# Key features of two blocks: transposed by VectorE and moved by DMA inside SBUF instead of transposed by TensorE, in a fused attention and gated-FFN layer

## The chip, the cores and the metric

The kernel runs on one core of a Trainium2 chip. Its metric is the device time of one launch in microseconds. Before the change the median of three runs is 671.38 us (670.75 to 671.44). A profile is one execution of its own, recorded by the hardware profiler; its times are counted from the start of the recorded span.

## What is computed

A sequence of 2048 tokens with 448 features is normalised, and the result is `x + A(xn) + B(xn)`. `A` is an attention with 16 heads of 28 features that goes through four blocks of 512 tokens and carries a memory `M` and its normaliser `z` from block to block; `B` is a gated feed-forward layer with 1792 hidden features.

```python
xn = layernorm(x)
for s in range(4):                       # blocks of 512 tokens
    qs, ks, vs = q[:, :, s], k[:, :, s], v[:, :, s]
    a_dot = softmax(qs @ ks.T * scale + mask) @ vs
    pq = phi(qs)                         # t + 1 where t > 0, exp(t) elsewhere
    a_mem = (pq @ M) / (pq @ z + 1e-6)
    o = g * a_mem + (1 - g) * a_dot
    pk = phi(ks)
    M = M + pk.T @ vs                    # the memory update
    z = z + pk.sum(tokens)
out = x + concat(o) @ wo + (sigmoid(xn @ w_gate) * (xn @ w_up)) @ w_down
```

## The kernel before, in words

Every matrix product is done with split operands: a value is a high part (rounded by ScalarE's copy to the type that TensorE reads fast) and a low part (the value less its high part), and a product is 11 matmuls of 128 rows each, the list `TERMS`. `xs0` to `xs3` hold the normalised tokens of the four blocks, transposed, in 7 chunks: 0 to 2 are high parts of 128 features, 4 to 6 their low parts, and chunk 3 holds the high part of the last 64 features in its upper 64 partitions and the low part in the lower 64. So matmuls 2, 3, 5, 6, 8 and 9 of a product touch a low part of tokens or weights, and the last two take chunk 3.

There is a front stage (some 140 us), in which the memory path and the projections are done, and then the long stage in which gated matmuls and causal attention are woven into each other. The change is in the front stage. It goes through the blocks `b` = 0 to 3 in the order in which the code stands:

- `values(b, t)` (L400) makes the value rows of one tile of 128 tokens (11 matmuls into a bank `pv`, then a copy by ScalarE into `vst`). Four tiles make a block.
- `keys_queries(b, c)` (L407) projects chunk `c` of the 896 key and query columns (11 matmuls into a bank `pp`; ScalarE makes the high part and the exponential, VectorE the low part `qk` and the feature map `e`). Chunks 0 to 3 hold keys, 3 to 6 queries. `qk` is stored to HBM (`qd`) for the attention, and the query features `e` to `fd`.
- `key_rows(c, e)` (L430) turns a key chunk so that tokens lie on partitions: four transposes by TensorE into a bank `pk`, and a copy by ScalarE into `kn`.
- `update(b)` (L438) adds the block's keys times values to the memory: 64 small matmuls into a bank `pmm` (keys stationary), then four VectorE instructions, one for each strip of 32 partitions, into `mst`.
- `recall(b, phi)` (L462) reads the memory of the blocks so far for the queries of a block: 32 small matmuls from `phi`, which SyncE loads back from `fd` (`load_features`, L459).
- For blocks 2 and 3 the normalised tokens are transposed by VectorE in squares of 32 by 32 (L359, into a staging buffer that is the space of `phi` for block 2 and of `acc2` for block 3), spread by 16 DMAs (L374, half on the queue of SyncE, half on that of GpSimd) into `stage`, and then split by `split_strips` (L377): ScalarE makes the high part, VectorE the low part.
- For block 1 the tokens are normalised by VectorE (L350) and transposed by TensorE (`pt`, L103). `statistics(2)` (L587) works out mean and variance of block 2's rows on VectorE.

TensorE, ScalarE and VectorE do the front stage's instructions in the order of the code. GpSimd's and SyncE's are put in an order by the tile framework's scheduler. Each engine takes its own instructions strictly in order; so a DMA that waits on SyncE's queue holds all DMAs behind it.

Of the kernel before, what the change touches and what calls it, by code (L numbers as in the profile page):

```python
# [9 lines left out]
F32 = mybir.dt.float32  # L10
# [6 lines left out]
P = 128  # L17
# [47 lines left out]
FILLS = (2, 2)  # L65
WARM = 10
# [3 lines left out]
def kernel(  # L70
# [236 lines left out]
    with tc.tile_pool(name="front", bufs=2) as sb, tc.manual_schedule(engines=FRONT):  # L307
# [69 lines left out]
        def split_strips(b, k):  # L377

            if k < 3:
                A.activation(xs[b][:, k, :], stage[:, k, :], AF.Copy)  # L380
                V.tensor_sub(xs[b][:, 4 + k, :], stage[:, k, :], xs[b][:, k, :].bitcast(F32))
            else:
                A.activation(xs[b][:64, 3, :], stage[:64, 3, :], AF.Copy)
                V.tensor_sub(xs[b][64:, 3, :], stage[:64, 3, :], xs[b][:64, 3, :].bitcast(F32))
# [52 lines left out]

        def update(b):  # L438

            pmm = bank("pmm", "m")  # L440
            for j in range(HG):
                for t in range(NT):
                    for i in range(NG):
                        h = HG * i + j
                        T.matmul(pmm[32 * i:32 * i + DH, 32 * j:32 * j + 32], kn[:, t, DH * h:DH * (h + 1)],  # L445
                                 vst[:, t, h, :], start=t == 0, stop=t == NT - 1)
            p3 = pmm[:, :P].rearrange("p (j c) -> p j c", c=32)
            new, old = mst[(b + 1) % 2], mst[b % 2]
            for i in range(NG):
                strip = slice(32 * i, 32 * i + DH)  # L450
                if b == 0:
                    V.tensor_copy(new[strip], p3[strip])
                else:
                    V.tensor_add(new[strip], p3[strip], old[strip])
# [4 lines left out]
        def load_features(b, i, phi):  # L459
            nc.sync.dma_start(phi[32 * i:32 * i + DH], fd[b][i * GW:(i + 1) * GW].rearrange("(j r) n -> r j n", r=DH))  # L460
# [28 lines left out]
        nc.sync.dma_start(stage[:, 0:2, :], w_qk[0:2].rearrange("c p n -> p c n"))  # L489
        nc.sync.dma_start(stage[:, 2:4, :], w_qk[2:4].rearrange("c p n -> p c n"))  # L490
        raw_qk = [stage[:, c, :] for c in range(4)]
        for c in range(4, 6):
            raw_qk.append(two_k("wqk_raw"))
            nc.sync.dma_start(raw_qk[c], w_qk[c])
        nc.sync.dma_start(acc[1], x_block(1))
        raw_qk.append(four_k(F32, "wqk_raw")[:, 0, :])
        nc.sync.dma_start(raw_qk[6], w_qk[6])
# [12 lines left out]
        def split_qk(c):  # L510
            r = raw_qk[c].rearrange("p (c n) -> p c n", c=4)
            A.activation(wqk[c][:, 0:4, :], r, AF.Copy)
            G.tensor_sub(wqk[c][:, 4:8, :], r, wqk[c][:, 0:4, :].bitcast(F32))
# [59 lines left out]
        for b in range(NB):  # L573
# [6 lines left out]
            for t in range(3 if b == 0 else 0, NT):  # L580
                values(b, t)
                if b == 0:
                    split_qk(t)
# [18 lines left out]
            for k, c in enumerate((3, 4, 5, 6, 0, 1, 2) if last else range(7)):  # L602
# [9 lines left out]
                if b == 0 and c + 4 < 7:  # L612
                    split_qk(c + 4)
                if b == 2 and 0 < n < NG or last and 0 < n <= NG:
                    answer(b - 1, n - 1, ts)
                if b == 2 and k == 6:
                    answer(1, NG - 1, ts)
                if k == 0:
                    if b == 0:
                        st[1] = rstd(*st[1])  # L620
                    if b == 0:
                        A.activation(gate, gate, AF.Exp, scale=-1.0)
# [6 lines left out]
                if last:  # L629
# [4 lines left out]
                    for i in range(NG):  # L634
                        if k == (2, 3, 4, 4)[i]:
                            load_features(b, i, phi)
# [6 lines left out]
                if k == 6:  # L643
                    update(b)
# [29 lines left out]
    class Pair:  # L674
# [5 lines left out]
        def load(self):  # L680

            self.qk = sb.tile([P, 2, 2, L], F32R, name="qk2", bufs=2)
            for c, parts in enumerate(((0, 0), (1, 0), (0, 1))):
                for n in range(2):
                    r0 = D * (1 - n) + DH * self.h0
                    nc.sync.dma_start(self.qk[DH * c:DH * (c + 1), n].bitcast(F32),
                                      qd[self.s][r0:r0 + 2 * DH, parts[n], :].rearrange("(j p) f -> p j f", p=DH))
# [268 lines left out]
```

## Time and profile before

| | |
|---|---|
| median of three runs | 671.38 us |
| the profiled execution: its time, and its span | 671.5 us, 669.6 us |
| TensorE busy | 663.7 us, 99% of the span |
| VectorE, ScalarE, GpSimd busy | 571.4, 336.1 and 147.4 us |
| DMA, mean over the span | 132 GB/s |

A profile's page gives the busy time of each engine, the chain of work that ended last, and groups of equal instructions with their count, mean duration in ns and the idle time before them. Its views by time give the start and length of single instructions or of runs of equal ones. PE is TensorE, DVE VectorE, ACT ScalarE, POOL GpSimd; SPq is the queue on which SyncE issues DMAs. L412 is line 412 of the kernel.

### The profile page before, as it was taken

Reading aid. Unit: us, or ns where it says so; the run is one execution under the profiler, and the core shown is the slowest. Engines: PE = TensorE matmul, PEld = TensorE weight load, DVE = VectorE, ACT = ScalarE, POOL = GpSimd, SP = SyncE. Lnnn points to the kernel's source line nnn. Section 1 sums busy time; section 2 is a strip of 40 time slices with the busy share of each in tenths; the row PEclk is TensorE's granted clock in tenths of the full one; section 3 lists DMA queues with packets and bytes.
Section 4 is the critical chain, followed back from the end, with each engine's and each line's share of the span. In section 5 each row is a group of like instructions: output and inputs, shape, how many; then the busy total and the mean of one; then the engine's idle time right before and its main releaser. Section 6 shows DMA issues by size and latency. Waiting matters only on the chain.

```text
span 669.6 us, 11201 instructions
## 1 busy us (share of the span) xinstructions
PE 663.7 (99%) x3922; PEld 553.2 (83%) x3922; DVE 571.4 (85%) x987; ACT 336.1 (50%) x560; POOL 147.4 (22%) x354
## 2 busy tenths in 40 slices
PE   8999999999999999999999999999999999999997
PEld 7888888778888888788787878788887887888897
DVE  6986695878999899899998999899998997999864
ACT  4848474423556455455645546455544644545220
POOL 3502210002222222233122322222122122321000
PEclk9999999999999999999999999999999999999999
DMA  8537788995523432324243423426243352323442
GB/s 321 221 128 251 238 287 284 309 273 197 144 73 88 109 93 73 103 57 105 74 96 103 89 72 57 128 52 141 57 103 64 92 115 57 86 78 80 112 153 97
DMA packets 48767, 88.09 MB, mean 132 GB/s; under 512 B 6856, under 2 KB 22856, under 8 KB 48200
## 3 DMA queue, kind: packets, MB, share of 16 engines
q1 hardware_dynamic: 45048, 79.01, 39.1%
q0 software_dynamic: 3520, 8.26, 6.1%
q8 instruction: 31, 0.51, 0.3%
q14 instruction: 24, 0.20, 0.1%
q10 hardware_dynamic: 144, 0.11, 0.0%
HBM read 52.89 MB, written 32.64 MB: 128 GB/s over the span
## 4 chain that ended last, share of the span: by engine, by line
PE 97%; DVE 2%; DMA 0%; ACT 0%; issue 0%; DVEq 0%
PE pgu L260 42%; PE pd L184 21%; PE pp L412 11%; PE st L704 6%; PE pa L790 5%; PE po L889 5%; PE pv L392 5%; PE pk L434 1%; PE pmm L445 1%; PE n L467 1%; DMA acc<-in_x 0%; DVE stats L324 0%; PE pt L103 0%; DVE xn L350 0%; DVE xs L110 0%
## 5 line engine op out<-in xcount | busy, mean ns | idle before, releaser
L260 PE MATMUL pgu<-xs,wgu 128*128 128x512 f32 x1232 | 301.2, 392 | 0.0
L260 PEld LDWEIGHTS pgu<-xs,wgu 128*128 128x128 f32 x1232 | 228.7, 188 | 46.6 <-issue 2.5
L184 PE MATMUL pd<-wdn,hh 128*128 128x448 f32 x672 | 155.3, 366 | 0.0
L184 PEld LDWEIGHTS pd<-wdn,hh 128*128 128x128 f32 x672 | 122.7, 188 | 11.6 <-issue 0.8
L719 POOL TENSOR_SCALAR_AFFINE_SELECT w<-w 128x256 f32<-128x256 f32 (+1 forms) x160 | 76.1, 479 | 224.0 <-ACT w L708 157.6
L772 ACT ACTIVATE w<-w 128x1024 f32<-128x1024 f32 (+1 forms) x96 | 87.8, 915 | 58.3 <-DVE w L768 58.1
L708 ACT ACTIVATE w<-st 128x512 f32<-128x512 f32 x128 | 75.6, 592 | 60.1 <-PE st L704 59.8
L768 DVE TENSOR_TENSOR w<-w,mb 128x1024 f32<-128x1024 f32 (+1 forms) x96 | 100.6, 1054 | 0.8
L726 DVE TRANSPOSE_TENSOR_REDUCE mx<-w 128x32 f32<-128x1024 f32 x64 | 78.9, 1233 | 4.9 <-POOL w L719 4.9
L412 PE MATMUL pp<-xs,wqk 128*128 128x512 f32 x308 | 73.7, 393 | 0.2 <-DVE kn L473 0.2
L186 DVE TENSOR_TENSOR acc<-pd,acc 128x448 f32<-128x448 f32 x112 | 67.4, 602 | 4.0 <-PE pd L184 4.0
L283 ACT ACTIVATE hh<-sg 128x512 fp32r<-128x512 f32 x56 | 35.3, 631 | 67.7 <-DVE sg L277 44.6
L412 PEld LDWEIGHTS pp<-xs,wqk 128*128 128x128 f32 x308 | 57.2, 188 | 12.9 <-issue 0.8
L704 PE MATMUL st<-qk 84*128 84x128 f32 (+3 forms) x256 | 62.0, 313 | 0.0
L267 ACT ACTIVATE sg<-pgu 128x512 f32<-128x512 f32 x56 | 33.2, 592 | 45.0 <-PE pgu L260 44.9
L704 PEld LDWEIGHTS st<-qk 84*128 84x128 f32 x256 | 47.9, 189 | 8.7 <-issue 1.4
L277 DVE SCALAR_TENSOR_TENSOR sg<-sg,pgu 128x512 f32<-128x512 f32 x56 | 37.7, 673 | 10.1 <-PE pgu L260 9.9
L754 DVE STREAM_TRANSPOSE mb<-top 128x1024 f32<-128x1024 f32 x32 | 39.5, 1234 | 3.3 <-POOL top L751 3.2
L286 DVE SCALAR_TENSOR_TENSOR hh<-sg,hh 128x512 fp32r<-128x512 f32 x56 | 38.2, 681 | 0.2 <-ACT hh L283 0.2
L419 DVE TENSOR_TENSOR qk<-pp,qk 128x512 fp32r<-128x512 f32 x28 | 19.2, 686 | 22.2 <-ACT e L417 21.6
L790 PE MATMUL pa<-w,vv 128*32 128x128 f32 (+3 forms) x512 | 37.8, 436 | 0.0
L392 PE MATMUL pv<-wv,xs 128*128 128x448 f32 x176 | 37.4, 367 | 0.3 <-POOL wv L508 0.2
(113 smaller groups left out, 607.2 us busy)
## 6 DMA issues: line engine op xcount, KB each, us to landing
qk<-qd SPq DMA_DIRECT2D x192, 112.0 KB
qd<-qk SPq DMA_DIRECT2D x28, 512.0 KB
raw<-in_w_ffn SPq DMA_DIRECT2D x14, 512.0 KB
acc<-in_x SPq DMA_DIRECT2D x5, 896.0 KB
vd<-vst SPq DMA_DIRECT2D x4, 1024.0 KB
vv<-vd SPq DMA_DIRECT2D x16, 256.0 KB
od<-w POOLq DMA_DIRECT2D x16, 256.0 KB, 4.1
sums<-od SPq DMA_DIRECT2D x32, 128.0 KB
```

The lines of the kernel that those rows point to most:

```text
L184: T.matmul(pd[:, :D], l, r, start=n == 0, stop=n == len(mms) - 1)
L186: V.tensor_add(acc[b][:, t, :], pd[:, :D], acc[b][:, t, :])
L260: T.matmul(dst, wgu[f][:, w, side * P:(side + 1) * P], xs[b][:, a, :], start=n == 0, stop=n == len(TERMS) - 1)
L392: T.matmul(pv[:, :D], xs[b][:, a, t * P:(t + 1) * P], wv[w], start=n == 0, stop=n == len(TERMS) - 1)
L412: T.matmul(pp, wqk[c][:, w, :], xs[b][:, a, :], start=n == 0, stop=n == len(TERMS) - 1)
L704: T.matmul(st[:, at:at + L - kb * P], self.qk[:KS, 1, h, kb * P:(kb + 1) * P], self.qk[:KS, 0, h, kb * P:], start=True, stop=True)
L708: A.activation(w, st, AF.Copy)
L719: G.affine_select(d, d, pattern=pattern, base=0, channel_multiplier=-1, compare_op=ALU.is_ge, fill=MASK)
L726: V.tensor_reduce(self.mx[:, 32 * h:32 * h + 32], w3[:, h, :2 * L].rearrange("p (b n) -> p b n", n=32), axis=mybir.AxisListType.X, op=ALU. ...
L768: V.tensor_sub(w, w, m)
L772: A.activation(w, w, AF.Exp, scale=SCALE)
L790: T.matmul(pa[32 * j:32 * j + 32, kb * P:], self.vv[:, kb, 32 * j:32 * j + 32], self.pairs[j // 2].block(j % 2, kb), start=kb == 0, stop=k ...
```

## The change

For blocks 1 and 2 (`EXCHANGED`) the key chunks no longer go through TensorE. VectorE transposes each chunk in squares of 32 by 32 into the staging buffer of the block after next (free by then), and 24 DMAs a block, half of them on SyncE's queue and half on GpSimd's, bring the squares to the partitions where the tokens belong, into `kn_blocks`. So that a head's features lie in a few squares, the columns of the key and query weights are put in another order (feature first, head second), on the chip: the weights come in eight DMAs with pieces of 512 bytes, and `split_qk` reads them with a step of 28 elements. Loads of `qd` and `fd` follow the new order.

`update` now has the values stationary and the keys moving, with a step of 16 elements between them; the sum is kept transposed in `memory` and turned by VectorE into `mst`. For blocks 1 and 2 it is called after the matmuls of the next block's first value tile. The low parts in `split_strips` go from VectorE to GpSimd. `statistics(2)` moves from ahead of block 0's keys to behind its second chunk; `split_qk` and some calls of `answer` (the memory's part of the output) move by a chunk or so.

```diff
+EXCHANGED = (1, 2)
...
+        memory = sb.tile([P, HG, 32], F32, name="memory", bufs=1)
         kn = eight_k(F32, "kn").rearrange("p (t a) n -> p t (a n)", t=NT)
+        kn_blocks = kn.rearrange("p t n -> p (t n)")[:, :NT * D].rearrange("p (m t r) -> p m t r", t=NT, r=32)
...
             if k < 3:
                 A.activation(xs[b][:, k, :], stage[:, k, :], AF.Copy)
-                V.tensor_sub(xs[b][:, 4 + k, :], stage[:, k, :], xs[b][:, k, :].bitcast(F32))
+                G.tensor_sub(xs[b][:, 4 + k, :], stage[:, k, :], xs[b][:, k, :].bitcast(F32))
...
         def values(b, t):
             pv = bank("pv", "p")
             value_terms(b, t, pv, EARLY[1] if b == 0 else TERMS)
+            if t == 0 and b - 1 in EXCHANGED:
+                update(b - 1)
             store_values(b, t, pv)
...
+        def turned(b, c):
+
+            space = stages[b + 1].rearrange("p (c n) -> p c n", n=256)
+            return space[:, 2 * c:2 * c + 2, :].rearrange("p c n -> p (c n)")
+
+        def turn_keys(e, et):
+            rows = et.shape[0]
+            V.transpose(et.rearrange("p (q t r) -> p t q r", q=4, t=NT),
+                        e[:rows].rearrange("p (t q n) -> p t q n", q=4, t=NT))
+
+        def send_keys(b, et=None):
...
+            for q in range(4):
+                for i in range(4 if et is None else 2):
+                    queue = nc.sync if i % 2 else nc.gpsimd
...
+                        queue.dma_start(to[32 * q:32 * q + 32, i:12:4, :], src[strip, :, q, :])
...
+                        queue.dma_start(to[32 * q:32 * q + 32, 12 + i, :], et[strip, P * q:P * (q + 1)])
+
+        def exchange(b, c):
+            if c == 1:
+                turn_keys(e[0], turned(b, 0))
+            elif c == 2:
+                turn_keys(e[1], turned(b, 1))
+                turn_keys(e[2], turned(b, 2))
+                send_keys(b)
+            elif c == 3:
+                et = sb.tile([P, L], F32, name="e", bufs=4)
+                turn_keys(e[3], et[:64])
+                send_keys(b, et)
...
-                        T.matmul(pmm[32 * i:32 * i + DH, 32 * j:32 * j + 32], kn[:, t, DH * h:DH * (h + 1)],
-                                 vst[:, t, h, :], start=t == 0, stop=t == NT - 1)
...
+                        T.matmul(pmm[32 * i:32 * i + 32, 32 * j:32 * j + DH], vst[:, t, h, :], rows[t][h],
+                                 start=t == 0, stop=t == NT - 1)
...
+                V.tensor_add(m3, p3, m3)
+            V.transpose(mst[(b + 1) % 2].rearrange("p j c -> p (j c)"), memory.rearrange("p j c -> p (j c)"))
...
+                r = raw_qk[side].rearrange("p w (h r) -> p w r h", h=H)[:, :, r0:r1, :]
...
-                    st[2] = statistics(2, 0, NT)
...
+                if b == 0 and k == 1:
+                    st[2] = statistics(2, 0, NT)
...
-                if k in (3, 5):
+                if b in EXCHANGED:
+                    exchange(b, c)
+                elif k in (3, 5):
```

How this moves instructions shows in three places. The first is VectorE in block 0, at its second chunk: `qk` and `e` are that chunk's low part and feature map, `xn` the first normalised tile of block 1, `acc_71` the rows of block 2. Before:

```order
L625 TENSOR_SCALAR gate_n<-gate 128x4
L419 TENSOR_TENSOR qk<-pp,qk 128x512
L424 SCALAR_TENSOR_TENSOR e<-pp,e 128x512
L350 TENSOR_SCALAR xn<-acc_70,mv_327,y_338 128x16x7x4
L419 TENSOR_TENSOR qk<-pp,qk 128x512
```

And now:

```order
L424 TENSOR_TENSOR qk<-pp,qk 128x512
L429 SCALAR_TENSOR_TENSOR e<-pp,e 128x512
L327 BN_STATS stats_397<-acc_71 128x6
L328 BN_AGGR mv_398<-stats_397 128x2
L327 BN_STATS stats_397<-acc_71 128x6
L328 BN_AGGR mv_398<-stats_397 128x2
L327 BN_STATS stats_397<-acc_71 128x6
L328 BN_AGGR mv_398<-stats_397 128x2
L327 BN_STATS stats_397<-acc_71 128x6
L328 BN_AGGR mv_398<-stats_397 128x2
L329 TENSOR_SCALAR vh_399<-mv_398 128x4
L353 TENSOR_SCALAR xn<-acc_70,mv_327,y_338 128x16x7x4
```

Nine instructions of `statistics(2)` have come between the chunk's feature map and the first normalised tile of block 1.

The second place is GpSimd's queue, and TensorE's, from block 2 to block 3 (`acc_71` is now the staging buffer, `xs_68` the tokens of block 3, `od` the attention's output in HBM). GpSimd before:

```order
L374 DMA stage<-acc_71 32x4x128
L374 DMA stage<-acc_71 32x3x128
L479 DMA od_92<-tb 128x512 x2
L479 DMA od_92<-xn 128x512 x2
L479 DMA od_93<-tb 128x512 x2
```

GpSimd now:

```order
L377 DMA stage<-acc_71 32x4x128
L377 DMA stage<-acc_71 32x3x128
L523 DMA od_92<-tb 128x512
L384 TENSOR_TENSOR xs_68<-stage,xs_68 128x512 x2
L462 DMA kn<-acc_71 32x3x128 x8
L464 DMA kn<-e 32x128 x4
L523 DMA od_92<-tb 128x512
L384 TENSOR_TENSOR xs_68<-stage,xs_68 128x512
L387 TENSOR_TENSOR xs_68<-stage,xs_68 64x512
L523 DMA od_92<-xn 128x512 x2
```

Twelve DMAs of the keys stand between the second and the third low part of block 3's tokens, and one more DMA. From block 1 to block 2 the twelve stand between the first low part and the second. TensorE there before (`xs_67` is block 2):

```order
L412 MATMUL pp<-xs_67,wqk_117 128x512 x11
L434 MATMUL pk<-ident,e 128x128 x8
L412 MATMUL pp<-xs_67,wqk_118 128x512 x11
L412 MATMUL pp<-xs_67,wqk_119 128x512 x11
L434 MATMUL pk<-ident,e 128x128 x8
L412 MATMUL pp<-xs_67,wqk_120 128x512 x11
L445 MATMUL pmm<-vst,kn 28x32 x64
L392 MATMUL pv<-wv,xs_68 128x448 x44
```

TensorE now:

```order
L417 MATMUL pp<-xs_67,wqk_117 128x512 x11
L417 MATMUL pp<-xs_67,wqk_118 128x512 x11
L417 MATMUL pp<-xs_67,wqk_119 128x512 x11
L417 MATMUL pp<-xs_67,wqk_120 128x512 x11
L395 MATMUL pv<-wv,xs_68 128x448 x11
L490 MATMUL pmm<-kn,vst 32x28 x64
L395 MATMUL pv<-wv,xs_68 128x448 x33
```

The transposes `pk` are gone, and the first value tile of the next block has moved ahead of the update.

The third place is SyncE's queue from block 1 to block 2 (`fd_84` holds block 1's query features, `phi` their reloaded copy, `vd_89` block 2's values). Before:

```order
L427 DMA fd_84<-e 128x512
L460 DMA phi<-fd_84 28x4x512
L420 DMA qd_80<-qk 128x1024
L427 DMA fd_84<-e 128x512
L460 DMA phi<-fd_84 28x4x512 x3
L398 DMA vd_89<-vst 128x2048
L374 DMA stage<-acc_71 32x4x128
L374 DMA stage<-acc_71 32x3x128
```

And now:

```order
L432 DMA fd_84<-e 128x512
L425 DMA qd_80<-qk 128x1024
L432 DMA fd_84<-e 128x512
L377 DMA stage<-acc_71 32x4x128
L503 DMA phi<-fd_84 28x2048 x4
L401 DMA vd_89<-vst 128x2048
L377 DMA stage<-acc_71 32x3x128
```

The first DMA of block 3's token spread, which needs all four normalised and turned tiles of block 3, has moved ahead of the loads of `phi`.

More of the change, by code (lines that the diff above doesn't have):

```diff
@@ L444, in update @@
                         h = HG * i + j
-                        T.matmul(pmm[32 * i:32 * i + DH, 32 * j:32 * j + 32], kn[:, t, DH * h:DH * (h + 1)],
-                                 vst[:, t, h, :], start=t == 0, stop=t == NT - 1)
[L447 to L454, printed above, removed]
+                        T.matmul(pmm[32 * i:32 * i + 32, 32 * j:32 * j + DH], vst[:, t, h, :], rows[t][h],
+                                 start=t == 0, stop=t == NT - 1)
+            p3, m3 = pmm[:, :P].rearrange("p (j c) -> p j c", c=32)[:, :, :DH], memory[:, :, :DH]
+            if b == 0:
+                V.tensor_copy(m3, p3)
+            else:
+                V.tensor_add(m3, p3, m3)
+            V.transpose(mst[(b + 1) % 2].rearrange("p j c -> p (j c)"), memory.rearrange("p j c -> p (j c)"))
         def features():
@@ L459, in load_features @@
         def load_features(b, i, phi):
-            nc.sync.dma_start(phi[32 * i:32 * i + DH], fd[b][i * GW:(i + 1) * GW].rearrange("(j r) n -> r j n", r=DH))
+            nc.sync.dma_start(phi[32 * i:32 * i + DH],
+                              fd[b].rearrange("(r h) n -> r h n", h=H)[:, HG * i:HG * (i + 1), :])
         def recall(b, phi):
@@ L488 @@
         raw = [raw[t // 2][:, t % 2 * D:(t % 2 + 1) * D] for t in range(4)]
[L489 to L497, printed above, removed]
+        raw_qk = [space.rearrange("p t n -> p (t n)")[:, :4 * D].rearrange("p (w n) -> p w n", w=4)
+                  for space in (stage, features())]
+        for side in range(2):
+            for c in range(4):
+                to, at = (P * c, 0) if side == 0 else (max(P * c - 64, 0), 64 if c == 0 else 0)
+                n = min(P, D - to) if side == 0 else P - at
+                nc.sync.dma_start(raw_qk[side][:, :, to:to + n],
+                                  w_qk[c + 3 * side].rearrange("p (w n) -> p w n", w=4)[:, :, at:at + n])
+            if side == 0:
+                nc.sync.dma_start(acc[1], x_block(1))
         load_rows(2)
@@ L510, in split_qk @@
         def split_qk(c):
-            r = raw_qk[c].rearrange("p (c n) -> p c n", c=4)
-            A.activation(wqk[c][:, 0:4, :], r, AF.Copy)
-            G.tensor_sub(wqk[c][:, 4:8, :], r, wqk[c][:, 0:4, :].bitcast(F32))
+            for side in range(2):
+                j0, j1 = max(P * c, D * side), min(P * (c + 1), D * (side + 1))
+                if j0 >= j1:
+                    continue
+                r0, r1 = ((j - D * side) // H for j in (j0, j1))
+                r = raw_qk[side].rearrange("p w (h r) -> p w r h", h=H)[:, :, r0:r1, :]
+                hi, lo = (wqk[c][:, w:w + 4, j0 - P * c:j1 - P * c].rearrange("p w (r h) -> p w r h", h=H)
+                          for w in (0, 4))
+                A.activation(hi, r, AF.Copy)
+                G.tensor_sub(lo, r, hi.bitcast(F32))
         warm = bank("warm", "gu")
@@ L611 @@
                     turn_back(n2, ts, range(2, NG))
[L612 to L617, printed above, removed]
+                if b == 0 and c + 3 < 7:
+                    split_qk(c + 3)
+                if b == 0 and k == 1:
+                    st[2] = statistics(2, 0, NT)
+                if b == 2 and k in (1, 4, 5, 6):
+                    answer(1, max(k - 3, 0), ts)
+                if last and 0 < n <= NG:
+                    answer(2, n - 1, ts)
                 if k == 0:
@@ L633 @@
                         phi = features()
-                    for i in range(NG):
-                        if k == (2, 3, 4, 4)[i]:
-                            load_features(b, i, phi)
+                    for i in range(NG if k == 4 else 0):
+                        load_features(b, i, phi)
                     if k > 4:
@@ L684, in load @@
                 for n in range(2):
-                    r0 = D * (1 - n) + DH * self.h0
-                    nc.sync.dma_start(self.qk[DH * c:DH * (c + 1), n].bitcast(F32),
-                                      qd[self.s][r0:r0 + 2 * DH, parts[n], :].rearrange("(j p) f -> p j f", p=DH))
+                    rows = qd[self.s][D * (1 - n):D * (2 - n), parts[n], :].rearrange("(r h) f -> r h f", h=H)
+                    nc.sync.dma_start(self.qk[DH * c:DH * (c + 1), n].bitcast(F32), rows[:, self.h0:self.h0 + 2, :])
         def block(self, h, kb):
```

16 lines of the change are left out of this document (13 added, 3 removed).

## The prediction

> **What bounds the kernel now.** I read the page first: busy shares, then the shares of the chain that ended last.
>
> ```profile
> PE 663.7 (99%) x3922; PEld 553.2 (83%) x3922; DVE 571.4 (85%) x987; ACT 336.1 (50%) x560; POOL 147.4 (22%) x354
> PE 97%; DVE 2%; DMA 0%; ACT 0%; issue 0%; DVEq 0%
> ```
>
> TensorE is busy for 663.7 of 669.6 us and makes 97% of the chain. Each stall that the change puts into TensorE's order lengthens the kernel, and each TensorE instruction that goes shortens it, as long as nothing else is late in its place. Then the chain of waits in the front stage (start, length, what, both in us):
>
> ```profile
> 19.84 9.98 PE pp L412 x44
> 29.82 1.05 PE pk L434 x8
> 30.87 0.48 PE pt L103 x4
> ...
> 51.27 10.00 PE pp L412 x44
> 61.27 0.87 PE pk L434 x8
> ...
> 67.17 0.87 PE pk L434 x8
> 68.04 2.52 PE pp L412 x11
> 70.56 1.22 PE pmm L445 x82
> 71.78 9.07 PE pv L392 x44
> 80.85 2.52 PE pp L412 x11
> 83.37 1.15 PE n L467 x32
> ...
> 92.23 0.87 PE pk L434 x8
> ...
> 98.12 0.87 PE pk L434 x8
> ```
>
> One TensorE piece follows the other without a gap. A chunk of keys or queries takes 2.50 to 2.52 us, a value tile 9.07/4 = 2.27, a matmul of it 0.21. So TensorE's clock is the clock of the front stage, and the question is which operand comes too late for it once the change is in.
>
> **What goes.** The four groups of `pk` in blocks 1 and 2, 0.87 us each, all on the chain: **-3.5 us**. That they do go is seen in TensorE's order, so "the change does nothing" is no case here. The update keeps its 64 matmuls.
>
> **Block 0: statistics(2) ahead of a normalised tile.** Rows of the timeline (VectorE, then ScalarE):
>
> ```profile
> 21.34 0.62 DVE L324 BATCH_NORM_STATS2 stats<-acc 128x6 f32<-128x448 f32 x1
> ...
> 24.39 0.17 DVE L326 TENSOR_SCALAR vh<-mv 128x4 f32<-128x4 f32 x1
> 24.59 0.69 DVE L419 TENSOR_TENSOR qk<-pp,qk 128x512 fp32r<-128x512 f32 x1
> ...
> 30.08 0.50 DVE L350 TENSOR_SCALAR xn<-acc,mv,y 128x448 f32<-128x448 f32 x1
> 23.55 0.59 ACT L417 ACTIVATE e<-pp 128x512 f32<-128x512 f32 x1
> ```
>
> The nine instructions hold VectorE from 21.34 to 24.59, 3.25 us. At their old place they delayed only L419, which could have begun when ScalarE's L417 ended (24.14): leaving gains at most 0.45. At the new place they stand straight ahead of L350 at 30.08. TensorE's `pt` at 30.87 needs that tile, ready at 30.58: 0.29 us of slack. Behind the waiting `pt` stands all of TensorE. 3.25 - 0.45 - 0.29 = **+2.5 us**; between 1.0 (if VectorE makes up more of its backlog earlier) and 3.2 (if the early gain isn't realised).
>
> **The low parts on GpSimd, at block 2's first value tile.**
>
> ```profile
> 60.60 0.69 DVE L424 SCALAR_TENSOR_TENSOR e<-pp,e 128x512 f32<-128x512 f32 x1
> L513 POOL TENSOR_TENSOR wqk<-stage,wqk 128x512 fp32r<-128x512 f32 x4 | 5.1, 1297 | 4.8 <-ACT wqk L512 4.8
> L374 POOL DMA_DIRECT2D stage<-acc x8 | 4.4, 558 | 26.2 <-ACT vst L396 26.2
> L478 DVE STREAM_TRANSPOSE tb<-phi 128x512 f32<-128x512 f32 x2 | 1.4, 711 | 0.1
> ```
>
> The first is a timeline row (chunk 2's feature map), the others are groups by shape: mean ns of one behind the comma. GpSimd needs 558 ns for each DMA that it issues and 1.3 us for a low part of 128x512 (the same operation as here). Chunk 2's map is there at 61.29, two turns of 0.71 follow: 62.7. Then 8 issues to 67.2, 4 more to 69.4, and behind them three low parts: 70.7, 72.0, 73.3. TensorE, without `pk`, ends its seven chunks at 51.27 + 7 x 2.50 = 68.8 and the value tile at 71.05. But the tile's last two matmuls take chunk 3, the third low part: the end is 73.3 + 2 x 0.21 = 73.7. **+2.7 us**; 1.8 if the low part takes 1.0 us in place of 1.3, 3.3 if a turn takes 0.99 (the dearer transpose shown below).
>
> **The recall of block 1's queries, through `phi`.**
>
> ```profile
> L454 DVE TENSOR_TENSOR mst<-pmm,mst 28x128 f32<-28x128 f32 x8 | 2.2, 281 | 0.1
> 74.20 0.51 DVE L350 TENSOR_SCALAR xn<-acc,mv,y 128x448 f32<-128x448 f32 x1
> ...
> 78.62 0.99 DVE L359 STREAM_TRANSPOSE acc<-xn 128x448 f32<-128x448 f32 x1
> L374 SPq DMA_DIRECT2D stage<-acc x8: 598/613/1581, 81.9 to 88.6; - x8
> L460 SPq DMA_DIRECT2D phi<-fd x12: 307/329/1712, 70.4 to 132.3; - x12
> DMA to landing us min/median/max: 1.9/3.0/4.9
> od<-tb POOLq DMA_DIRECT2D x6, 256.0 KB, 5.0
> od<-xn POOLq DMA_DIRECT2D x6, 256.0 KB, 4.0
> ```
>
> (The fourth and fifth are issues on SyncE's queue, least, median and longest ns; the sixth is the landing of `stage` transfers, the last two that of `od` ones.) The update now ends at 73.7 + 1.22 = 74.9; VectorE adds (0.28) and turns (at most 0.3): 75.5. The four normalised and turned tiles took from 74.20 to 79.61, 5.4 us, and now end at 80.9. On SyncE's queue the first `stage` DMA, which needs all four, has moved ahead of the loads of `phi`, so those wait for VectorE: 81.5 behind its 0.6; the fourth load is issued at 81.5 + 3 x 0.33 = 82.5. Loads of 224 KB have no landing time in the views; 256 KB took 4.0 to 5.0: 86.5 to 87.5, and a quarter of the recall (0.3) comes after the last strip: 86.8 to 87.8. TensorE wants to begin the recall at 73.7 + 1.22 + 6.8 + 2.52 = 84.2 and end it at 85.4. I take the upper part, 87.7, because the spread's transfers share the engines then: **+2.3 us**; nothing with the least landing (1.9), 3.8 with 5.0 and one issue of 1.71.
>
> **The low parts again, at block 3's first value tile.**
>
> ```profile
> 62.43 0.63 ACT L418 ACTIVATE e<-e 128x512 f32<-128x512 f32 x1
> L479 POOL DMA_DIRECT2D od<-tb x4 | 2.2, 557 | 32.6 <-DVE tb L478 32.6
> ```
>
> After the recall at 87.7 come chunks 1 to 6: chunk 3 ends at 95.3, chunk 6 at 102.8, the tile unstalled at 105.1. The high part of the second strip follows chunk 3's exponential by one ScalarE copy: in block 1 that is chunk end 61.27, exponential 63.06, copy some 0.55 later, so 2.3 us after the chunk; here 97.6. GpSimd: that strip's low part to 98.9, 8 issues to 103.4, 4 to 105.6, one `od` DMA to 106.2, two low parts to 107.5 and 108.8; the tile ends at 109.2. **+4.1 us**, 3.2 to 4.6 with a low part at 1.0 or an issue at 0.59.
>
> **What I cost at nothing.** VectorE's four turns a block (2.8 us) take the place of its four low parts:
>
> ```profile
> L381 DVE TENSOR_TENSOR xs<-stage,xs 128x512 fp32r<-128x512 f32 x6 | 4.1, 681 | 1.0 <-ACT xs L380 0.8
> stage<-acc POOLq DMA_DIRECT2D x4, 64.0 KB, 4.4
> ```
>
> 0.68 each, 2.7 us. The squares' DMAs on both queues: GpSimd's last issue at 69.4 plus the 4.4 us that a like transfer took is 73.8, when the update may begin at 73.7; that is a tie, and SyncE's half is issued alongside. Without this cover the update waits 1 to 2 us more. The query and key weights in pieces of 512 bytes: first needed at 19.84, and `split_qk` on ScalarE and GpSimd lies beside the value matmuls; no row shows such pieces, so 0 to +1. ScalarE loses its `kn` copies, which nobody waited for.
>
> **The sum.** -3.5 + 2.5 + 2.7 + 2.3 + 4.1 = +8.1 us. The profiled execution took 671.5 us (span 669.6), so 679.6 and a span of 677.7; the median of the runs is 0.1 below it: **679.5**. Behind the front stage TensorE's order is unchanged and busy, so nothing is won back there.
>
> **Rivals.**
> 1. GpSimd's queue doesn't hold (the other side). If the next instruction begins before a DMA issue's 558 ns are over, the low parts come in time. At the first place that needs 62.7 + 12 issues + 3.9 by 70.6: 0.33 us each; at the second 98.9 + 13 issues + 2.6 by 104.7: 0.25. Below that both waits go, -6.8: 672.8 with the recall as above and 670.5 with none. For it: these issues make no data wait in the views. Against it: groups of eight lie end to end at 558 ns (8 in 4.4 us).
> 2. A step between the update's moving elements costs. The update's keys are now read with a step of 64 bytes. The nearest row is the transpose whose writes are strided: 0.99 for 448 columns against 0.711 for 512, 1.6 times a column. At 1.22 us an update that is +0.7 each, three on the chain: 681.6. Against it: a matmul of 28 columns is so short that its weight load may cover it. [...]
> 3. TensorE's clock falls in the new gaps.
>
> ```profile
> 103.00:140.00 37.00, 36.80 (x215) 28.68 (x213) 24.92 (x47) 15.10 (x26) 2.70 (x5) 1.00 0.87 297
> L518 PE MATMUL warm<-ident 128*128 128x128 f32 x20 | 4.6, 429 | 1.4 <-POOL ident masks.py:199 1.4
> L521 PE MATMUL warm<-ident 128*128 128x128 f32 x10 | 1.3, 278 | 0.0
> ```
>
> The granted clock (the 1.00) is full, and TensorE never rests long in the front stage. At the start the same matmul went from 429 to 278 ns, 1.54 times. The longest new gap, at block 3's tile, is about 3 us (some 103.9 to 107.5 with one matmul between). If the clock falls there for 3 to 6 us of work: +1.7 to 3.4, about 682. [...]
>
> **How the numbers follow.** Forecast 0.57, rival 1 0.14, rival 2 0.14, rival 3 0.10, the rest 0.05. The terms' low ends give 671.5 - 3.5 + 1.0 + 1.8 + 0 + 3.2 = 674.0, the high ones 671.5 - 3.5 + 3.2 + 3.3 + 3.8 + 4.6 = 682.9; all ends at once are unlikely, and rivals 2 and 3 add 2 to 3 at the top: 674.5 to 685.0. That leaves out rival 1 and little else. 0.2%, 1.3 us, is about what a measurement of this kernel can tell from no change. Rival 1 divides into faster 0.05, same 0.06 and slower 0.03; the rest adds 0.02 faster and 0.01 same; slower is 0.86.
>
> **What would show it.** `pk` of blocks 1 and 2 missing from TensorE's rows, 3.5 us; `pt` in block 0 waiting for `xn` by 2.5 us; `pv` of blocks 2 and 3 waiting for GpSimd's low parts by 2.7 and 4.1 us, with twelve DMA issues of 558 ns ahead of them; the recall of block 1's queries waiting for a `phi` load issued behind the first `stage` DMA, 2.3 us; clock 1.00 throughout. I am wrong if GpSimd's low parts stand ahead of their use, if one takes much less than 1.3 us, or if the update's keys land later than the value tile.

## The result, and the profile after

The changed kernel takes 692.95 us (median of five runs, 692.5 to 694.38) against 670.83 us before: 1.033 times as long, interval 1.032 to 1.035. That is 22 us more; 8.1 were forecast, and the range ended at 685. The profiled execution has a span of 691.2 us, 21.6 more than before. From the page, busy shares and the chain that ended last:

```profile
PE 672.7 (97%) x3890; PEld 555.2 (80%) x3890; DVE 572.8 (83%) x982; ACT 336.4 (49%) x553; POOL 173.1 (25%) x387
PE 80%; DMA 4%; DVE 3%; issue 1%; ACT 1%; SPq 0%; DVEq 0%; ACTq 0%
```

TensorE has 32 instructions fewer and yet is busy 9 us longer, and other engines and DMAs have come into the chain. (The views below have two records for each matmul of an update and of a recall: the 64 of an update appear as x128 and the 16 that the code of a recall has as x32, 8 for each strip of 32 partitions.) The view of waits of TensorE in the first 165 us (who was waited for, us in total, times, longest) names them; before, TensorE waited for 0.2 us in all between 14 and 165 us:

```profile
PE pv L395 <- POOL xs L384: 4.4, 3, 3.0
PE pt L104 <- DVE xn L353: 3.4, 2, 2.9
PE n L511 <- DMA phi<-fd: 2.5, 4, 1.0
PE pv L395 <- POOL xs L387: 1.5, 2, 0.9
PE pp L417 <- POOL wqk L565: 0.7, 1, 0.7
```

The first four lines are the places of the forecast; their idle time is 11.8 us, of which 0.6 (a `pt` at 8.5 us) and 1.0 (the last recall, at 160 us) lie elsewhere. The fifth is a wait of block 0's chunk 3 for the low part of its weights. The rest is in how long TensorE's work takes. Its timeline (start, length, instruction; in brackets the idle time ahead of it), blocks 0 to 3:

```profile
34.84 0.71 PE L104 MATMUL pt<-ident,xn 128*128 128x128 f32 x4 [2.87 <-DVE xn L353]
...
44.80 1.82 PE L490 MATMUL pmm<-kn,vst 128*32 128x28 f32 x128
...
55.85 17.64 PE L417 MATMUL pp<-xs,wqk 128*128 128x512 f32 x77
73.33 1.17 PE L395 MATMUL pv<-wv,xs 128*128 128x448 f32 x5
75.51 0.88 PE L395 MATMUL pv<-wv,xs 128*128 128x448 f32 x3 [1.01 <-POOL xs L384]
...
78.09 1.12 PE L395 MATMUL pv<-wv,xs 128*128 128x448 f32 x2 [0.88 <-POOL xs L387]
79.14 1.93 PE L490 MATMUL pmm<-kn,vst 128*32 128x28 f32 x128
...
87.90 2.68 PE L417 MATMUL pp<-xs,wqk 128*128 128x512 f32 x11
91.46 1.06 PE L511 MATMUL n<-phi,mst 28*32 28x512 f32 x8 [0.88 <-DMA phi<-fd]
92.77 2.25 PE L511 MATMUL n<-phi,mst 28*32 28x512 f32 x16 [0.25 <-DMA phi<-fd]
95.43 1.93 PE L511 MATMUL n<-phi,mst 28*32 28x512 f32 x8 [0.42 <-DMA phi<-fd]
97.29 17.42 PE L417 MATMUL pp<-xs,wqk 128*128 128x512 f32 x66
114.55 1.77 PE L395 MATMUL pv<-wv,xs 128*128 128x448 f32 x8
119.31 0.74 PE L395 MATMUL pv<-wv,xs 128*128 128x448 f32 x1 [3.00 <-POOL xs L384]
```

Three things beside the waits are to be seen. An update (`pmm`) takes 1.82 to 1.93 us. The recall (`n`) comes in pieces, and each group of 8 takes 1.06 or more by itself. Before, in the same view:

```profile
70.49 1.29 PE L445 MATMUL pmm<-vst,kn 128*28 128x32 f32 x128
...
83.30 1.22 PE L467 MATMUL n<-phi,mst 28*32 28x512 f32 x32
```

The third is the clock. The 66 matmuls at 97.29 take 17.4 us, where the 77 at 55.85 take 17.6. The view by stretches of time shows it (the granted clock is the third number from the end):

```profile
98.00:102.00 4.00, 4.00 (x11) 3.13 (x10) 2.48 (x5) 0.00 (x0) 0.00 (x0) 0.51 0.52 180
102.00:106.00 4.00, 4.00 (x19) 3.26 (x19) 2.54 (x6) 2.92 (x6) 0.00 (x0) 1.00 0.31 114
...
122.00:126.00 4.00, 3.69 (x133) 3.51 (x134) 3.86 (x9) 1.58 (x3) 0.55 (x1) 0.53 1.01 380
```

From 98 to 102 us TensorE does 11 matmuls in the time of 19.

What the four waits are made of stands in the queues. First VectorE and GpSimd in block 0 (timeline):

```profile
21.48 1.19 DVE L329 TENSOR_SCALAR vh<-mv 128x4 f32<-128x4 f32 x1
19.45 3.18 POOL L565 TENSOR_TENSOR wqk<-stage,wqk 128x512 fp32r<-128x512 f32 x2 [0.83 <-ACT wqk L564]
```

The instruction of four elements that the prediction shows took 0.17 us. Here it takes 1.19 and ends at 22.67, within 0.04 us of the end of a GpSimd subtraction (22.63); the next of its kind, at 33.47, takes 0.90 and ends at 34.37 beside another (34.34). Then the timeline of VectorE's last feature map of block 1 and of SyncE's queue of DMAs from block 1 to block 2:

```profile
77.80 0.69 DVE L429 SCALAR_TENSOR_TENSOR e<-pp,e 128x512 f32<-128x512 f32 x1
67.31 5.11 SPq L462 DMA_DIRECT2D kn<-phi  x8
...
73.76 2.86 SPq L464 DMA_DIRECT2D kn<-e  x4
...
80.61 0.60 SPq L432 DMA_DIRECT2D fd<-e  x1
87.12 0.65 SPq L377 DMA_DIRECT2D stage<-acc  x1
88.19 1.63 SPq L503 DMA_DIRECT2D phi<-fd  x4
```

Twelve issues of squares hold SyncE for 8 us, and the stores of `qk` and `e` stand between and behind them. So buffers for `e` come free late, and ScalarE waits for them, as its view of waits from 50 to 165 us says (twice, 7.9 us in total):

```profile
ACT e L422 <- DMA fd<-e: 7.9, 2, 5.5
```

Chunk 6's last matmul ends at 73.33; its features are done at 78.5 and stored at 80.61, 7.3 us behind the matmul.

### The profile page after: what moved, and what is told of

It reads as the page before. It is cut to its first block, busy times and chain, and to the rows that moved or that the text cites. A ratio compares the mean times of both kernels' runs of the same rounds, so it can differ in the third digit from the quotient of the medians.

```text
span 691.2 us, 11246 instructions
## 1 busy us (share of the span) xinstructions
PE 672.7 (97%) x3890; PEld 555.2 (80%) x3890; DVE 572.8 (83%) x982; ACT 336.4 (49%) x553; POOL 173.1 (25%) x387
## 4 chain that ended last, share of the span: by engine, by line
PE 80%; DMA 4%; DVE 3%; issue 1%; ACT 1%; SPq 0%; DVEq 0%; ACTq 0%
PE pgu L261 40%; PE pd L185 20%; PE st L757 6%; PE pa L843 5%; PE po L942 5%; DMA phi<-fd 2%; PE pp L417 2%; DMA fd<-e 1%; DVE acc L362 1%; DVE e L429 1%; PE n L511 1%; DVE qk L424 0%; DMA qd<-qk 0%; ACT e L422 0%; SPq L503 0%
## 5 line engine op out<-in xcount | busy, mean ns | idle before, releaser
L417 PE MATMUL pp<-xs,wqk 128*128 128x512 f32 x308 | 75.3, 401 | 0.7 <-POOL wqk L565 0.7
L417 PEld LDWEIGHTS pp<-xs,wqk 128*128 128x128 f32 x308 | 59.0, 193 | 15.5 <-issue 1.7
L395 PE MATMUL pv<-wv,xs 128*128 128x448 f32 x176 | 41.4, 385 | 6.1 <-POOL xs L384 4.4
L278 DVE SCALAR_TENSOR_TENSOR sg<-sg,pgu 128x512 f32<-128x512 f32 x56 | 37.7, 674 | 10.3 <-PE pgu L261 10.2
L395 PEld LDWEIGHTS pv<-wv,xs 128*128 128x128 f32 x176 | 33.4, 197 | 11.4 <-POOL xs L384 5.5
```

The source lines that it names most:

```text
L395: T.matmul(pv[:, :D], xs[b][:, a, t * P:(t + 1) * P], wv[w], start=n == 0, stop=n == len(TERMS) - 1)
L417: T.matmul(pp, wqk[c][:, w, :], xs[b][:, a, :], start=n == 0, stop=n == len(TERMS) - 1)
```

## Experiments

From the changed kernel's profile three theories stood against each other. **A**: the time is lost by what stands ahead of a needed instruction in GpSimd's queue and VectorE's, and by clock falls that follow the waits. **B**: the squares' transfers take the DMA engines, whatever the queues. **C** joined A after the first four runs: SyncE's queue does for the stores and `phi` what GpSimd's does for the low parts. All kernels are the changed kernel with the edit shown, some with more than one change at once, which is said there; before, on the same chips, took 670.98 to 671.37 us.

### Low parts back on VectorE

```diff
-                G.tensor_sub(xs[b][:, 4 + k, :], stage[:, k, :], xs[b][:, k, :].bitcast(F32))
+                V.tensor_sub(xs[b][:, 4 + k, :], stage[:, k, :], xs[b][:, k, :].bitcast(F32))
...
-                G.tensor_sub(xs[b][64:, 3, :], stage[:64, 3, :], xs[b][:64, 3, :].bitcast(F32))
+                V.tensor_sub(xs[b][64:, 3, :], stage[:64, 3, :], xs[b][:64, 3, :].bitcast(F32))
```

> The changed kernel with the low parts of split_strips back on VectorE; everything else as in the change. Theory A (what stands in a queue): the waits of the value tiles of blocks 2 and 3 (2.2 and 4.1 us of TensorE idle) are made by GpSimd's low parts standing behind its twelve DMA issues; they go, and the falls of the granted clock that follow them (0.57 at 78 to 82 us, 0.53 to 0.62 at 118 to 126) go too: 6.3 of idle plus about 2 of slow clock, 684 to 686 us. Theory B (the squares' transfers take the DMA engines, whatever the queues): the waits move to the transfers, the time stays within 689 to 693 us.

Measured: 692.32 us (689.88 to 694.97), 1.032 of before (1.029 to 1.035). A's 684 to 686 did not come. TensorE's timeline of this kernel says why:

```profile
73.29 2.37 PE L395 MATMUL pv<-wv,xs 128*128 128x448 f32 x11
77.87 1.93 PE L490 MATMUL pmm<-kn,vst 128*32 128x28 f32 x128 [2.21 <-DMA kn<-e]
...
117.63 0.67 PE L395 MATMUL pv<-wv,xs 128*128 128x448 f32 x2 [3.28 <-DVE xs L387]
```

In block 2 the value tile runs through, and the update behind it waits 2.21 us for the squares: the one wait had covered the other. In block 3 the low part is as late as on GpSimd, since VectorE's own queue is full there: its timeline has no gap from 104.03 (a turn of keys) to 117.58 (the low part that was waited for).

### statistics(2) at its old place

```diff
                     A.activation(one, ident[:, 0:1], AF.Exp)
+                    st[2] = statistics(2, 0, NT)
...
-                if b == 0 and k == 1:
-                    st[2] = statistics(2, 0, NT)
```

> The changed kernel with statistics(2) back ahead of block 0's keys. Theory A: pt of block 0 no longer waits for xn (2.9 us), all later parts shift: 689 to 690 us. If the wait of pt came from GpSimd's splits of the weights holding VectorE (VectorE's rows of 4 elements that took 0.8 to 1.2 us in place of 0.17) and not from the place of the statistics, only about 1 us is won: 692 us. Theory B: as A, no statement on this part.

Measured: 689.17 us, 1.027 (1.025 to 1.030): 3.8 us less than the changed kernel. `pt` starts at 32.00 instead of 34.84 us, without the 2.87 us of wait. The place of the statistics is the cause; what is left against before (30.71) is 1.3 us, of which 0.66 is the wait for the weights' low part (at 28.42 here).

### phi's loads ahead of the spread on SyncE

```diff
-            nc.sync.dma_start(phi[32 * i:32 * i + DH],
+            return nc.sync.dma_start(phi[32 * i:32 * i + DH],
...
-                    load_features(b - 1, i, phi)
+                    load = load_features(b - 1, i, phi)
...
-                        spread(3)
+                        with tc.issue_after(load):
+                            spread(3)
```

> The changed kernel with the four loads of phi for block 1's queries put ahead of the first stage DMA on SyncE's queue. Theory A: the recall in block 2 loses its waits (1.55 us), its four strips run side by side again (4 us less) and the clock does not fall behind it (2.3 us in the next chunk): 685 to 688 us. Theory B: the loads share the engines with other transfers and still come late; at most 1.5 us is won: 691.5 to 693 us.

Measured: 690.82 us (688.42 to 693.72), 1.028 (1.025 to 1.031); about 2 us less, between the two expectations, and its runs lie 5 us apart. SyncE's timeline:

```profile
82.02 0.60 SPq L432 DMA_DIRECT2D fd<-e  x1
87.43 1.62 SPq L503 DMA_DIRECT2D phi<-fd  x4
```

Nothing stands between the last store and the loads now, and still they go out 5.4 us after it: they read what that store writes, and the store itself goes out late. From the last matmul of chunk 6 to the loads it was 14.9 us in the changed kernel and is 12.6 here; without exchange (next) it is 5.7. So the place behind the `stage` DMA is the smaller part of the loads' delay. For the recall it weighed more: it ends 3.2 us after chunk 0 here instead of 6.8, though in the longest of the four runs, with clock falls elsewhere.

### No block exchanged

```diff
-EXCHANGED = (1, 2)
+EXCHANGED = ()
```

> The changed kernel with no block exchanged: keys of all blocks turned by TensorE, no turns and no squares' transfers; the order of the weights, the low parts on GpSimd, statistics(2), phi's place and the new update stay. Theory A: without twelve issues ahead of them the low parts come in time, -6.3 of idle and -2 of slow clock, against +3.5 for pk; the recall stays late and block 0 too: 687 to 689 us. Theory B: the recall's loads come sooner as well, -5 more: 682 to 684 us.

Measured: 682.53 us, 1.018 (1.016 to 1.019). That is B's number, not A's: the recall is on time as well. In this kernel the last store of `fd` goes out at 79.05 us, 2.6 us behind its chunk's last matmul (76.44), where the changed kernel needs 7.3, and the loads of `phi` at 82.10. So the exchange makes the recall late, either by its transfers or by its place in SyncE's queue. One more thing differs: the scheduler has put the loads of `phi` ahead of the spread here (88.34), as in the kernel before. The next two runs part these.

### Half of the squares left out

One kernel sends only GpSimd's half, the other only SyncE's.

```diff
-                for i in range(4 if et is None else 2):
+                for i in range(0, 4 if et is None else 2, 2):
```

(SyncE's half left out; in the other the range starts at 1.) The kernel without SyncE's half also clears the buffer of the keys at its start:

```diff
+        nc.gpsimd.memset(kn, 0.0)
```

> The changed kernel without the half of the squares that SyncE issues: that half of the keys of blocks 1 and 2 is not moved (the buffer is cleared once at the start, so old values stand there), all else stays. Theory C (SyncE's queue): its twelve issues of 0.64 to 0.74 us a block stand ahead of the stores of qk and e, so the last fd store goes out some 6 us after its data, and with it the loads of phi; and ScalarE waits 7.9 us for e buffers. Without them the recall of block 2 has no wait and its strips run side by side, the clock does not fall there: 5 to 8 us won, 685 to 688 us; the waits of the value tiles for GpSimd's low parts stay. Theory B (the transfers themselves): both halves cost alike, each leaving out gives about 3 us, at the value tiles as well as at the recall.

> The changed kernel without the half of the squares that GpSimd issues (that half of the keys of blocks 1 and 2 is not moved). Theory A with C: GpSimd's low parts come 6 us sooner, the value tiles of blocks 2 and 3 no longer wait for them (4.4 + 1.5 us), the update then waits up to 2 us for SyncE's squares, and the recall stays late, since SyncE's queue is as before: 685 to 689 us. Theory B: about 3 us at both places, 690 us.

Without SyncE's half: 688.07 us, 1.025 (1.023 to 1.027), 4.9 us less. The recall in TensorE's timeline:

```profile
93.95 1.22 PE L512 MATMUL n<-phi,mst 28*32 28x512 f32 x32
```

No wait, all strips together, and the clock is 1.00 from 70 to 110 us, as C has it. The value tiles still wait for GpSimd as before. Here too the scheduler has put the loads of `phi` (83.93) ahead of the spread (92.57), so the kernel to compare with is that of the third experiment: from chunk 6's last matmul to the loads it is 6.4 us instead of 12.6. That is the part of SyncE's squares. (The clearing delays the first keys by 1.3 us, 21.15 instead of 19.83, so the gain would be larger without it.) Without GpSimd's half: 693.77 us, 1.035 (1.033 to 1.037), nothing won:

```profile
74.90 2.37 PE L395 MATMUL pv<-wv,xs 128*128 128x448 f32 x11
79.37 1.86 PE L490 MATMUL pmm<-kn,vst 128*32 128x28 f32 x128 [2.10 <-DMA kn<-e]
...
95.63 1.61 PE L511 MATMUL n<-phi,mst 28*32 28x512 f32 x16 [1.73 <-DMA phi<-fd]
...
121.73 1.93 PE L490 MATMUL pmm<-kn,vst 128*32 128x28 f32 x128 [4.26 <-issue]
```

The value tile of block 2 runs through and the update waits for SyncE's squares; the recall stays late. Block 3's update waits as well, 4.26 us, longer than the tile ahead of it did in the changed kernel (3.60). The bracket names nothing for it, but the view of the squares' transfers from `e` puts 6.4 us of the update's waiting, twice, down to them: 2.10 and 4.26. That is why nothing is won. SyncE needs 5.10 us for eight squares here and 5.11 with GpSimd's half beside it, so its issues are not slowed by the other half. As many transfers are left out as in the other kernel, with another result, so B as it was told falls: it matters whose queue they stand in. A share of the transfers in later landings is not ruled out: from the last store of `fd` to the loads that wait for it alone it is 5.4 us with all squares, 3.7 without SyncE's and 3.1 without exchange.

### No squares at all, with the turns kept

```diff
+        nc.gpsimd.memset(kn, 0.0)
...
-                for i in range(4 if et is None else 2):
+                for i in range(0):
```

> The changed kernel with the turns on VectorE kept and none of the 48 DMAs of squares issued (the keys of blocks 1 and 2 are not moved; the buffer is cleared once). Leaving out GpSimd's half alone gained nothing and SyncE's half alone about 5 us. Theory A with C, joined: each half hides the other at the value tiles (GpSimd's low parts, and the landing of the last squares behind SyncE's issues, come at nearly the same time), so that both have to go: no wait in the value tiles, at the update or the recall, the clock at 1.00 from 46 to 132 us, and the time is that of no_exchange less the 3.5 us of pk: 679 us, 678 to 680. If the turns on VectorE or the low parts on GpSimd cost something by themselves, value tiles still wait and it is 682 or more.

Measured: 678.91 us (678.63 to 679.25), 1.012 (1.010 to 1.013), in the middle of what was expected.

```profile
74.37 2.37 PE L396 MATMUL pv<-wv,xs 128*128 128x448 f32 x11
76.68 1.83 PE L491 MATMUL pmm<-kn,vst 128*32 128x28 f32 x128
...
87.76 1.22 PE L512 MATMUL n<-phi,mst 28*32 28x512 f32 x32
...
106.93 0.68 PE L396 MATMUL pv<-wv,xs 128*128 128x448 f32 x2 [0.95 <-POOL xs L388]
```

Value tile, update and recall of block 2 have no wait; the low part in block 3 costs 0.95 us by being on GpSimd. The 48 DMAs are worth 692.95 - 678.91 = 14.0 us, and a microsecond more if the clearing is counted, which lets the keys begin at 20.79 instead of 19.83. The loads of `phi` stand ahead of the spread here as well, so their place is in the 14.0. Against the kernel without exchange, 3.6 us less: the four groups of `pk` (blocks 1 and 2 are 1.9 us shorter each in TensorE's timeline; the rest of the difference is elsewhere and nearly cancels).

### The step between the update's keys

```diff
+            rows = [[kn[:, t, DH * h:DH * (h + 1)] for h in range(H)] for t in range(NT)]
...
-            if b in EXCHANGED:
-                rows = [[kn_blocks.rearrange("p m t (c h) -> p m t c h", h=H)[:, :, t, :, h] for h in range(H)]
-                        for t in range(NT)]
-            else:
-                rows = [[kn[:, t, h:D:H] for h in range(H)] for t in range(NT)]
```

> The changed kernel with the update reading 28 neighbouring columns as a head's keys in place of columns 16 apart (the memory is then summed over other features; the count and size of matmuls stay). If the step is what made an update 1.75 to 1.93 us in place of 1.22, it goes back to 1.2 to 1.3: 1.8 us less on the path, 691 us. If it is the new order (values stationary, 128 x 32 weights in place of 128 x 28), the update stays at 1.8 and the time at 693 us.

Measured: 694.19 us, 1.034 (1.033 to 1.036); no gain in the time. But block 0's update, at the full clock, is back at its old length:

```profile
46.26 1.29 PE L486 MATMUL pmm<-kn,vst 128*32 128x28 f32 x128
...
80.08 2.21 PE L486 MATMUL pmm<-kn,vst 128*32 128x28 f32 x128
```

So the step costs 0.53 us an update (1.82 to 1.29 in the same view). The two other updates fall where the changed kernel's clock is 0.50 (in the mean of 70 to 92 and of 110 to 132 us it is 0.92 and 0.84 in both kernels); there it takes 2.1 to 2.2 us without the step and 1.93 with it. Why the latter isn't the longer one was not found out, and the other microsecond in the median was not traced.

### Work put into TensorE's waits

```diff
+        def keep_busy(n):
+            spare = bank("spare", "s")
+            for _ in range(n):
+                T.matmul(spare, wqk[0][:, 0, :], xs[0][:, 0, :], start=True, stop=True)
...
+                for n, some in ((5, (4, 0)), (8, (1, 12)), (9, (3, 2))):
+                    value_terms(b, t, pv, TERMS, n0, n)
+                    if some[b - 2]:
+                        keep_busy(some[b - 2])
...
+                        if k == 3:
+                            keep_busy(11)
                         turn(1, k - 3, xn[k - 3])
```

> The changed kernel with matmuls on old data, their result unused, put into TensorE's waits: 11 ahead of the waiting pt of block 0, 4, 1 and 3 in the value tile of block 2, 12 and 2 in that of block 3, together about the length of each wait, so that nothing starts later by more than 0.3 us each. If idle TensorE is what lets the granted clock fall, it stays at 1.00 from 30 to 90 us and from 105 to 135 us, the work behind the value tiles of blocks 2 and 3 and behind pt runs at full speed, 2 to 4 us less (689 to 691 us) and the runs lie closer together than 2 us. If the clock falls for another reason the time stays at 693 us or goes up by the fillers.

Measured: 697.27 us (691.9 to 699.05), 1.037 (1.034 to 1.040): longer, and wider. In block 3, where the waits were filled, the clock held (stretches as above, the last line):

```profile
70.00:92.00 22.00, 18.82 (x197) 15.45 (x196) 9.69 (x16) 6.73 (x12) 9.85 (x15) 0.92 0.55 178
92.00:110.00 18.00, 17.40 (x78) 10.66 (x78) 7.17 (x13) 6.25 (x11) 3.19 (x7) 0.81 0.73 223
110.00:132.00 22.00, 21.07 (x216) 17.64 (x215) 16.15 (x29) 11.14 (x19) 13.52 (x20) 1.00 0.77 266
```

In the last stretch the changed kernel had 0.84, and block 3's four value tiles with the update take 15.5 us here (117.38 to 132.86) instead of 17.1. But inside block 2's update a stall of 2.37 us appeared for which the profile names nothing, the clock fell there and at the recall, which had not been filled, and the gain was more than lost. Idle time as the cause of the falls is supported by one place; as a cure the filling failed, and the stall's cause stays open.

### What is left without exchange, statistics and GpSimd's low parts

This joins the edits of the first, second and fourth kernel.

> The changed kernel with no block exchanged, the low parts back on VectorE and statistics(2) back ahead of block 0's keys: what is left is the order of the weights with their loads in pieces of 512 bytes and strided splits, the new update and phi's loads all at one place. Expected over before: three updates of 1.8 in place of 1.25 (+1.6), pt of block 0 1.3 later as in stats_back, the last recall 1.5 to 2 later: 671.4 + 4.7 = 676 us, 675 to 677. If the new order of the weights costs more in the attention (its loads of qd read rows 16 apart), it is 678 or more, and the excess lies behind 166 us.

Measured: 677.48 us (677.43 to 677.68), 1.010 (1.008 to 1.011), half a microsecond above the range expected. TensorE's timeline:

```profile
31.96 0.71 PE L104 MATMUL pt<-ident,xn 128*128 128x128 f32 x4 [0.19 <-DVE xn L353]
...
142.89 2.17 PE L511 MATMUL n<-phi,mst 28*32 28x512 f32 x16 [0.46 <-DMA phi<-fd]
```

Against before, `pt` is 1.25 us late (0.64 of it the wait for the weights' low part), three updates add 0.5 each, and the last recall waits for `phi` and comes in two parts, 1.7 us more; behind it the clock is at 0.95 from 132 to 166 us (1.00 before). What the new order of the weights costs in the attention can't be told apart from that clock.

No run points to a version that beats the kernel before: were all 48 DMAs free and all else put back, -3.5 for `pk` and +1.6 for the updates would leave 2 us at best.

## Why the prediction was wrong, step by step

The direction and the places were right, the size was not: 22 us instead of 8.

| step | forecast | shown |
|---|---|---|
| `pk` of blocks 1 and 2 gone | -3.5 | -3.6 (no_squares against no_exchange) |
| block 0, statistics(2) | +2.5 | +3.8 (stats_back) |
| value tiles and recall: GpSimd's queue and `phi` | +9.1 | +14.0 (no_squares; waits of the update and falls of the clock are in it) |
| the update with a step | 0 (rival: +2.1) | +1.6 (0.53 each) |
| the rest of rest_only: block 0, last recall | 0 (weights 0 to +1) | +4.9 |
| remainder: low parts on GpSimd without squares | in the terms above | +1.2 |

The remainder is worked out from no_squares against rest_only (678.9 - (677.5 - 3.6 + 3.8) = 1.2), so that the rows add up to 21.9 of the 22.1 us is no test of them.

TensorE's timelines of the two profiled executions can be set against the forecast place by place. `pt` starts 4.1 us later (2.5 forecast), block 2's first tile costs 3.6 (2.7), the recall 5.6 (2.3), block 3's first tile 5.0 (4.1). At nothing the forecast had the updates (1.8, and a wait of 0.5 ahead of one), the last recall (1.6) and the falls of the clock (3.1). Less 3.5 for `pk` that is 21.8, and the spans differ by 21.6.

**Value tiles.** The wait for GpSimd's low parts was there, with twelve issues ahead of it (4.35 and 1.99 us in the changed kernel, from 67.83 us on, and the low parts behind them from 74.18) as worked out, 3.6 us to the end of block 2's first tile instead of 2.7, and 5.0 to that of block 3's, above the 3.2 to 4.6 that were given. But the forecast's reason was half of it. It called the landing of the squares a tie and asked 1 to 2 us for it "without this cover": the kernels with low parts on VectorE, or without GpSimd's squares, paid 2.2 and 2.1 us there. Two causes that end at the same time can't be undone one by one, and the two attempts to undo one of them alone won nothing that stands out from the scatter.

**The recall.** This is the step that failed, with the largest excess of one place: +2.3 was forecast, and from the end of chunk 0 to that of the recall it was 6.8 us instead of 1.15. The path was the forecast one, and it did end last: SyncE waited 5.9 us for VectorE's tiles at the `stage` DMA, with the loads behind it. The chain of the changed kernel runs from the update through VectorE's four tiles and the `stage` DMA to the loads:

```profile
86.07 1.00 DVE acc L362
...
87.12 0.65 SPq L377
...
89.44 5.95 DMA phi<-fd
...
95.43 1.93 PE n L511 x8
```

From the update's end (81.1) to the fourth load's issue it took 8.3 us, 7.6 in the forecast. The sizes behind that were wrong: the load took 5.95 us instead of 5.0, and "a quarter of the recall (0.3) comes after the last strip" became 1.93, at half the clock. The 32 records took 1.15 us together before, the 8 of one strip 1.06 alone here, and in the kernel with the low parts on VectorE four strips that came one by one took 1.06, 1.06, 1.06 and 1.39 us. The forecast also missed a second path that ends some 2 us earlier. SyncE's half of the squares holds back the store from which `phi` is loaded, by 4.7 us (7.3 less 2.6); the order of SyncE's queue showed those twelve issues, and the working charged the issues to GpSimd alone ("SyncE's half is issued alongside"). So moving the loads alone won 2 us, and the recall was on time only in the kernels without SyncE's squares, which have the loads ahead of the spread as well.

**Block 0.** The statistics cost about what was said (`pt` waited 2.87). Ahead of that wait `pk` was already 1.3 us late: chunk 3's second matmul waited 0.66 for the low part of its weights, which GpSimd now makes in two instructions and ends at 28.44. That is in the 0 to +1 that the forecast gave to the weights in pieces and left out of its sum. Some of VectorE's small instructions also ended with GpSimd's subtractions (above, 1.19 and 0.90 us instead of 0.17). Before already showed that: instructions of four elements took 0.72 and 0.96 us there (at 26.00 and 28.01) and ended with GpSimd's subtractions at 26.7 and 28.95.

**The rivals.** GpSimd's issues do hold its queue: the second and third low part of block 2 began at 74.18 us, behind the last of the twelve issues, which ended at 74.16 (rival 1 fell). That a weight load may cover the step was not shown; the step cost 0.53 us an update. Rivals 2 and 3 both came true, with 0.14 and 0.10, and beside the forecast, not instead of it. Chances were given as if one of them could hold at a time; they are terms, and each makes the other's cover thinner.

**The clock.** In the changed kernel it is at one half from 78.0 to 81.4, from 95.1 to 101.9 and from 119.0 to 125.8 us, worked out from half-microsecond steps of the same view. Counted on the work in it: chunk 1 of block 2 takes 4.86 us in the chain instead of 2.52, and block 3's last three value tiles 7.6 in TensorE's timeline instead of no_squares' 6.9: 3.1 us, and some more at the recall. The three falls last 3.4, 6.8 and 6.8 us. The 3 to 6 us of work that rival 3 gave to a fall, and with it its share in the upper end of the range, were the author's estimate, which no run shows; the 3.1 us stand in their place. What lets the clock fall, and for how long, was not shown: the same wait of `pt`, 2.9 to 3.0 us in eight kernels with that part alike, was followed by a lower clock in five (0.83 to 0.91 from 26 to 46 us) and not in three (1.00).

## What to carry to other kernels

Work that leaves a busy engine lands in queues: count for every DMA the time on the queue that issues it, and go through everything behind it on that queue, the stores on whose landing a later load waits most of all. When a kernel runs without gaps on TensorE, reckon that a wait can cost more than itself (here 3.1 us of slow clock stood beside 10.2 us of waits at the four places), and rivals that can hold together are to be added, not weighed against each other. When an undone cause wins nothing, look for a second one that ends at the same time before dropping the theory.

## What the runs showed of the hardware

- The granted clock of the changed kernel fell to 0.50 at one wait of 3.00 us (block 3's tile, from 119.0), after waits of 1.01, 0.35 and 0.88 us with matmuls between them (block 2's tile, from 78.0) and of 0.88, 0.25 and 0.42 (the recall, from 95.1). In `rest_only` it was 0.95 in the mean from 132 to 166 us, where TensorE has a single wait of 0.46, at the recall. Kernels with several such places scatter: `stats_back` 688.0 to 691.7, `filled` 691.9 to 699.1. `no_squares`, with one wait of 3.00, and `rest_only` stay within 0.6 us. What makes the others scatter was not shown.
- SyncE took 0.64 to 0.73 us to issue a DMA of squares (5.11 and 5.86 us for eight), GpSimd 0.50 to 0.54 (1.99 us for four, 4.35 for eight).
- Four of VectorE's instructions of four elements, named above, took 0.72 to 1.19 us and ended within 0.04 us of the end of a GpSimd subtraction (22.67 beside 22.63 and 34.37 beside 34.34 in the changed kernel). Two others inside such subtractions kept 0.17 and 0.18 us (at 25.80 and 27.80 in the kernel before), and a `qk` subtraction kept its 0.65 us beside one of GpSimd's (at 107.56 in the changed kernel). What parts them was not shown.
- The step of 64 bytes between the moving elements cost 0.53 us in an update's 64 matmuls of 28 columns at the full clock (1.82 against 1.29 us).
